# Re-ordering the opening of a fused attention and MLP kernel, with a new table of scheduling offsets

## The chip, the cores and the metric

The kernel runs on one core of a Trainium2 chip. The metric is the device time of one execution in microseconds; the value shown is the median of several executions.

## The reference

The program is an attention with a learned bias of relative position, followed by a two-layer MLP on its output. Everything is float32.

```python
# q, k, v: (4, 8, 576, 64); w1 (1, 32), b1 (32), w2 (32, 8); w_in (512, 2048), w_out (2048, 512)
scores = scale * q @ k.T
x = log1p(|i - j|) / log1p(max(i, 1))
bias = relu(x * w1 + b1) @ w2            # one value for each (i, j, head)
attn = softmax(scores + bias) @ v
x = attn as (2304, 512)
out = relu(x @ w_in) ** 2 @ w_out
```

## The kernel before

**Attention.** There are 80 steps (`steps`), one for each of two pairs of batches, five chunks of query rows (`ORDER`; chunk 0 is the 64-row tail and comes first) and eight heads. A step runs `qk` (scores in the one PSUM tile `sc`, from Q and K split in two float16 parts each), `softmax_a` (DVE adds the bias tile `bt`, takes the maximum and writes `s`, L441; ACT exponentiates, L445 to L447), `softmax_b` (the transposes for the next product: on PE in the first two chunks, L459 to L463, by DMA later) and, three steps behind (`LAG`), `pv`. After eight heads `finish_x` scales and splits the rows for the MLP.

**Bias.** The bias is made in 36 groups of 16 query rows. `hgen` makes four hidden tiles `hg` of a group, some on ACT, some on DVE: L303 and L305 for the first four groups, L307 and L309 for the others. `bias_mm` multiplies them with `w2` on PE (L348), evicts the result with ACT or DVE (L369 to L374) and stores it to DRAM (L378, tensor `biasd`). `bias_ld` (L392, L394) reads it back in the skewed layout that a step needs. The first four groups multiply the table by the row's factor directly; the later ones use row factors `rows_s` and inverted factors `scl`, which `rowscale` (L324 to L334) makes once from the table `tab_t`.

**MLP.** `moe_unit` runs `g1` (L560) and, some units later, `g2` (L583). The weights come as 32 pieces; `WT.split` rebuilds the words of each piece on DVE (`ci`, `cv`; L223, L224, L226), casts the high part on ACT (through `cast`, L129) and makes the low part on POOL (L131, L242). Two pieces a step are split in most of the first 16 steps (`W_AT`). `KV.split` and `q_split` cast K and Q on POOL (L131, L189) and finish Q on DVE (L268).

**Order of the work.** The instructions of `with pinned()` keep the program's order on each engine. Those of `with behind()` follow them. Everything else is ordered by a scheduler when the program is built: among the instructions that are ready by its own simulated times it takes the one with the smallest priority number, which grows in program order. `place(kind)` adds an offset from `PLACE` to the instructions inside it while the step is below `PLACED` (26), so that a positive offset moves them behind later work: `softmax_a`, the hidden tiles and the high casts of the weights by 150, K and V loads by 80, `bias_mm` by 20, and `qk` ahead by 10. On the chip each engine and each DMA queue then runs its own list in order. All DMAs are issued on SP's queue.

**The opening** (L735 to L765) loads the small constants `sm_t`, the table, two weight pieces, Q and K, makes the first four groups, splits K and Q (`kv_split(0)`, `q_split`), splits two weight pieces, runs `rowscale`, makes the hidden tiles of the fifth group and issues the bias loads of the first two heads. Step 0 with its `qk` and `softmax_a` comes after that.

Of the kernel before, what the change touches and what calls it, by code (L numbers as in the profile page):

```python
# [13 lines left out]
ALU = mybir.AluOpType  # L14
# [29 lines left out]
PLACE = {'qk': -10, 'wh': 150, 'sa': 150, 'hg': 150, 'bm': 20, 'kd': 80}  # L44
PLACED = 26
# [6 lines left out]
def tile_attention_moe(  # L52
# [57 lines left out]
    rows_s = const.tile([128, 36], F32, name="rows_s")  # L110
    nb1 = const.tile([128, 1], F32, name="nb1")
# [24 lines left out]
    @contextmanager  # L136
    def place(kind):
        n = PLACE.get(kind, 0) if now[0] < PLACED else 0
        tc.cur_priority += n
        yield  # L140
        tc.cur_priority -= n
# [59 lines left out]
    class WT:  # L201
# [14 lines left out]
        def split(self):  # L216
# [18 lines left out]
            with place("wh"):  # L235
                cast(zn("wh", u), hi, st, float(2 ** e))
# [49 lines left out]
    def hgen(G, pl=None):  # L286
        ts_ = []
        for t in range(4):
# [12 lines left out]
            if groups.index(G) < 4:  # L301
                if hg_pat(G)[t] == "A":
                    nc.scalar.activation(out=ht, in_=src, func=AF.Relu, bias=sm_t[:, 1:2], scale=sclw[:, n - 128:n - 127])  # L303
                else:
                    nc.vector.tensor_scalar(ht, src, sclw[:, n - 128:n - 127], nb1, op0=ALU.mult, op1=ALU.max)  # L305
# [5 lines left out]
        hg[G] = ts_  # L311

    def hconst():
# [4 lines left out]
        for z in sorted({hg_z(G) for G in groups}):  # L318
            nc.vector.tensor_copy(hcst[:, z:z + 1], cp[:, 0:1])
            for t in range(4):  # L320
                if PATS[z][t] == "A":
                    nc.vector.memset(hcst[32 * t:32 * t + 32, z:z + 1], 0.0)

    def rowscale():  # L324
        cp = ps_h.tile([128, 512], F32, tag="h", name="cp")
        for t in range(4):
            nc.tensor.matmul(out=cp[32 * t:32 * t + 32, 0:36], lhsT=sel,
                             rhs=scl.rearrange("p (g t) -> p t g", t=4)[:, t, :],
                             start=True, stop=True, tile_position=(0, 32 * t))
        nc.vector.tensor_copy(rows_s, cp[:, 0:36])  # L330
        nc.vector.reciprocal(out=scl, in_=scl)
        nc.vector.tensor_scalar(scl, scl, sm_t[:, 1:2], None, op0=ALU.mult)
        nc.gpsimd.tensor_scalar(w2n, w2s, -1.0, 1.0, op0=ALU.mult, op1=ALU.mult)
        nc.scalar.activation(out=tab_t[:, 0:LW], in_=tab_t[:, 0:LW], func=AF.Identity, scale=hcst[:, 3:4], bias=0.0)  # L334

    def bias_mm(G, gi):
        ts_ = hg.pop(G)
        z = hg_z(G)
        D_ = dlen(G)
        F_, M_ = S - 16 * G, 16 * G + 16  # L340
        cuts = [0, D_] if D_ <= 512 else [0, 288, D_]
        for d0, d1 in zip(cuts[:-1], cuts[1:]):
# [4 lines left out]
            for t in range(4):  # L347
# [3 lines left out]
                                 start=True, stop=True, tile_position=(0, 32 * t))  # L351

# [30 lines left out]
    def bias_ld(p, c, h):  # L383
# [6 lines left out]
        if c == 0:  # L390
            for b in range(2):
                last = nc.sync.dma_start(out=t[64 * b:64 * b + 64, :], in_=rows(512, 64))  # L392
# [483 lines left out]
```

## Time and profile before

| what | value |
|---|---|
| three executions | 661.16, 658.57, 660.46 us |
| median | 660.46 us |
| the profiled execution: its own time | 661.45 us |
| its span, first to last instruction | 659.7 us |
| mean granted TensorE clock over the span | 0.965 |
| PE, DVE, ACT, POOL busy | 93%, 62%, 59%, 57% of the span |

PE is TensorE, DVE VectorE, ACT ScalarE, POOL GpSimd, and SP the queue that issues the DMAs. L12 is line 12 of the kernel before. A busy share is an average over the span, and stages differ: so stretches are read one by one. A granted clock of 1.00 is 2.4 GHz and of 0.50 is 1.2 GHz; values between are means over a stretch with both. The wait in square brackets in a timeline is the idle time of the engine before that instruction, with what ended it.

### The profile page before, as it was taken

How to read it: one execution, taken by the hardware profiler on the slowest of the kernel's cores; microseconds unless marked ns; L12 is line 12 of the kernel's file. 1: busy time of each engine (PE TensorE's matmuls, PEld its weight loads, DVE VectorE, ACT ScalarE, POOL GpSimd, SP SyncE). 2: the span in 40 equal slices, each digit the busy share in tenths (PEclk: the TensorE clock that was granted, in tenths of full speed). 3: DMA queues.
4: the chain of work that ended last, by engine and by line, in shares of the span. 5: the costliest groups of instructions: out<-in, count | busy, mean ns of one | idle time of the engine just before them, and what ended most of it. 6: DMA issues, size and time to landing. Idle time of an engine off the chain costs nothing.

```text
span 659.7 us, 15574 instructions
## 1 busy us (share of the span) xinstructions
PE 615.1 (93%) x6056; PEld 394.8 (60%) x6056; DVE 407.1 (62%) x813; ACT 388.1 (59%) x856; POOL 376.5 (57%) x394
## 2 busy tenths in 40 slices
PE   5565798999899999999899999999999999999997
PEld 2223356766455566666576676676676676767664
DVE  7997999888864765585856447346545642632321
ACT  5587978788776476656656655656465564342111
POOL 2757578899665456756775465555464663432221
PEclk9698967999999999999899999999999999999999
DMA  7999888477876787889978778679787777524000
GB/s 237 278 294 319 268 255 248 155 209 178 197 173 152 162 193 176 179 180 226 221 170 158 167 134 174 140 169 153 139 172 134 154 149 155 122 56 86 17 34 16
DMA packets 206568, 112.16 MB, mean 170 GB/s; under 512 B 167072, under 2 KB 183456, under 8 KB 206496
## 3 DMA queue, kind: packets, MB, share of 16 engines
q1 hardware_dynamic: 206496, 111.19, 72.0%
q8 instruction: 47, 0.77, 0.5%
q14 instruction: 25, 0.20, 0.1%
HBM read 55.44 MB, written 15.61 MB: 108 GB/s over the span
## 4 chain that ended last, share of the span: by engine, by line
PE 69%; DVE 5%; DMA 4%; issue 2%; ACT 1%; POOL 1%; DVEq 0%; POOLq 0%; ACTq 0%
PE o L583 26%; PE hp L560 26%; PE pv L506 8%; PE sc L425 5%; PE bp L348 2%; DMA at<-a 2%; DVE hg L309 1%; PE sc L419 1%; PE sc L413 1%; DMA xt<-xh 1%; DMA stg<-vd 1%; DVE s L441 1%; DVE cv L226 0%; DVE ci L224 0%; ACT a L129 0%
## 5 line engine op out<-in xcount | busy, mean ns | idle before, releaser
L560 PE MATMUL hp<-xt,winH 128*128 128x256 f16 (+1 forms) x1280 | 195.9, 263 | 0.0
L583 PE MATMUL o<-woutH,g 128*128 128x512 f16 x576 | 185.6, 382 | 4.0 <-ACT o L590 2.2
L560 PE MATMUL hp<-xt,winL 128*128 128x256 f16 (+1 forms) x640 | 162.8, 263 | 0.0
L583 PEld LDWEIGHTS <-g 128*128 128x128 f16 x864 | 82.8, 98 | 97.0 <-issue 11.5
L560 PEld LDWEIGHTS <-winH 128*128 128x128 f16 x1280 | 117.0, 99 | 30.0 <-issue 13.6
L441 DVE CUSTOM_DVE_ANT_0 s<-sc,bt 128x576 f32<-128x576 f32 x144 | 103.5, 751 | 44.1 <-PE sc L425 34.2
L474 POOL TENSOR_TENSOR a<-s,a 128x1024 f16<-128x1024 f32 (+1 forms) x64 | 130.3, 2036 | 0.0
L568 DVE TENSOR_TENSOR r<-hp,r 128x512 f32<-128x512 f32 (+1 forms) x80 | 50.6, 632 | 118.7 <-ACT r L566 118.6
L570 POOL TENSOR_TENSOR g<-r,g 128x512 f16<-128x512 f32 (+1 forms) x80 | 86.7, 1084 | 59.1 <-DVE g L133 48.4
L447 ACT ACTIVATE s<-s,nm 128x576 f32<-128x576 f32 x144 | 111.3, 773 | 6.4
L583 PE MATMUL o<-woutL,g 128*128 128x512 f16 x288 | 109.8, 381 | 0.0
L473 POOL TENSOR_TENSOR a<-s,a 128x128 f16<-128x128 f32 (+1 forms) x64 | 28.1, 440 | 140.4 <-ACT a L129 135.5
L445 ACT ACTIVATE nm<-mx,esc 128x1 f32<-128x1 f32 x144 | 40.9, 288 | 110.8 <-DVE mx L441 110.5
L506 PE MATMUL pv<-v,at 128*128 128x64 f16 (+5 forms) x2112 | 97.9, 207 | 0.5 <-ACT at L460 0.5
L129 ACT ACTIVATE a<-s 128x1152 f16<-128x1152 f32 (+1 forms) x64 | 70.5, 1102 | 44.6 <-DMA at<-a 43.6
L566 ACT ACTIVATE r<-hp 128x512 f32<-128x512 f32 (+1 forms) x80 | 43.1, 539 | 49.6 <-PE hp L560 49.6
L506 PEld LDWEIGHTS <-at 128*128 128x128 f16 (+1 forms) x1792 | 58.3, 100 | 20.2 <-issue 8.6
L560 PEld LDWEIGHTS <-winL 128*128 128x128 f16 x640 | 62.9, 98 | 5.8
L309 DVE TENSOR_SCALAR hg<-tab_t 128x464 f32<-128x464 f32 (+17 forms) x86 | 58.9, 729 | 11.5 <-PE bp L348 11.4
L425 PE MATMUL sc<-k,q 64*128 64x512 f16 x384 | 55.6, 387 | 0.0
L369 ACT ACTIVATE be<-bp,hcst,rows_s 128x288 f32<-128x288 f32 (+29 forms) x67 | 35.8, 571 | 16.5 <-PE bp L348 11.1
L348 PE MATMUL bp<-hg,w2s 128*32 128x288 f32 (+15 forms) x152 | 36.1, 546 | 6.1 <-ACT hg L303 2.4
(88 smaller groups left out, 688.7 us busy)
## 6 DMA issues: line engine op xcount, KB each, us to landing
bt<-biasd SPq DMA_DIRECT2D x64, 288.0 KB, 3.3
stg<-w_in SPq DMA_DIRECT2D x16, 512.0 KB, 5.1
stg<-w_out SPq DMA_DIRECT2D x16, 512.0 KB, 4.7
bt<-biasd SPq DMA_DIRECT2D x32, 144.0 KB, 3.4
qst<-qd SPq DMA_DIRECT2D x32, 128.0 KB, 3.5
out<-o SPq DMA_DIRECT2D x16, 256.0 KB, 2.4
v<-vd SPq DMA_DIRECT2D x8, 320.0 KB, 4.9
stg<-vd SPq DMA_DIRECT2D x8, 320.0 KB, 4.3
```

The lines of the kernel that those rows point to most:

```text
L129: nc.scalar.activation(out=out, in_=in_, func=AF.Copy, scale=scale)
L309: nc.vector.tensor_scalar(ht, src, scl[:, n:n + 1], None, op0=ALU.min)
L348: nc.tensor.matmul(out=bp[32 * t:32 * t + 32, 0:d1 - d0], lhsT=w2s if gi < 4 or PATS[z][t] == "A" else w2n, rhs=ts_[t][:, d0:d1], start=Tr ...
L425: nc.tensor.matmul(out=sc[:, 1024 * b:1024 * b + 512], lhsT=qt[r, qz, qs], rhs=kt[r, z, 64 * b:64 * b + 512], start=(n == 0), stop=(n == 2 ...
L441: nc.vector.tensor_tensor_reduce(s[:, 576 * b:576 * b + 576], sc[:, 960 * sb:960 * sb + 576], bt, inv, -3.0e38, ALU.add, ALU.max, mx[:, b: ...
L447: nc.scalar.activation(out=sl, in_=sl, func=AF.Exp, bias=nm[:, b:b + 1], accum_out=su[:, h, b:b + 1])
L474: nc.gpsimd.tensor_tensor(av[:, :, 640:1152], ev[:, :, 0:512], av[:, :, 0:512], op=ALU.subtract)
L506: nc.tensor.matmul(out=dst, lhsT=lhsT, rhs=vt[r, 5 * b + blk, :] if f32 else vt[:, vz, 5 * b + blk, :], start=(n == 0), stop=(n == nt - 1) ...
L560: nc.tensor.matmul(out=hp[:, f * T:f * T + T].rearrange("p (b t) -> p b t", b=nb), lhsT=wt[:, k, c0:c0 + 128], rhs=xt[:, 0:nb, z * 4 + k, ...
L568: nc.vector.tensor_tensor(rr, hp[:, 0:2 * T], rr, op=ALU.mult)
L570: nc.gpsimd.tensor_tensor(g[:, 1, 0:2 * T], r[:, 0:2 * T], g[:, 0, 0:2 * T], op=ALU.subtract)
L583: nc.tensor.matmul(out=blk["o"][b], lhsT=g[:, z, c0:c0 + 128], rhs=wt[:, 2 * u + f, :], start=(u == 0 and f == 0 and z == 0 and wt is wout ...
```

## The change

The opening is re-ordered, and the offsets are replaced.

- The table's DMA is issued ahead of that of `sm_t`. `w2s`, one column of `hcst` and `w2n` are made on POOL instead of DVE and POOL late. `hconst` makes the three columns of `hcst` with one product of a mask `hmask` and the PSUM column instead of copies and memsets, and also runs the four pairs of matmuls for `rows_s`, which ACT copies out.
- `bias_mm` is cut in `bias_pe` and `bias_ev`, and the evictions of a group come one group of hidden tiles later. The reciprocal and product that invert `scl` stand between evictions.
- The first K split is made to wait for the last DVE hidden tile of the fourth group.
- The bias loads of two heads come ahead of the two weight pieces, one half tile on ACT's queue; `qk` and `softmax_a` of step 0 join the pinned part, ahead of the fifth group's hidden tiles.
- `PLACE` now holds ranges of steps with an offset each; ranges add up.

```diff
-PLACE = {'qk': -10, 'wh': 150, 'sa': 150, 'hg': 150, 'bm': 20, 'kd': 80}
-PLACED = 26
+PLACE = {'qk': [(22, 30, -20)], 'hg': [(0, 26, 150), (15, 31, 80)], 'bm': [(0, 26, 20), (25, 26, 80), (17, 19, 150)], 'm': [(24, 28, 20), (15, 16, 80)], 'pv': [(9, 34, -10)]}
...
-        n = PLACE.get(kind, 0) if now[0] < PLACED else 0
+        n = sum(x for a, b, x in PLACE.get(kind, ()) if a <= now[0] < b)
...
-            with place("wh"):
-                cast(zn("wh", u), hi, st, float(2 ** e))
+            cast(zn("wh", u), hi, st, float(2 ** e))
...
     def hconst():
...
-        for z in sorted({hg_z(G) for G in groups}):
-            nc.vector.tensor_copy(hcst[:, z:z + 1], cp[:, 0:1])
-            for t in range(4):
-                if PATS[z][t] == "A":
-                    nc.vector.memset(hcst[32 * t:32 * t + 32, z:z + 1], 0.0)
-
-    def rowscale():
-        cp = ps_h.tile([128, 512], F32, tag="h", name="cp")
         for t in range(4):
-            nc.tensor.matmul(out=cp[32 * t:32 * t + 32, 0:36], lhsT=sel,
+            nc.tensor.matmul(out=cp[32 * t:32 * t + 32, 8:44], lhsT=sel,
...
-        nc.vector.tensor_copy(rows_s, cp[:, 0:36])
-        nc.vector.reciprocal(out=scl, in_=scl)
-        nc.vector.tensor_scalar(scl, scl, sm_t[:, 1:2], None, op0=ALU.mult)
-        nc.gpsimd.tensor_scalar(w2n, w2s, -1.0, 1.0, op0=ALU.mult, op1=ALU.mult)
-        nc.scalar.activation(out=tab_t[:, 0:LW], in_=tab_t[:, 0:LW], func=AF.Identity, scale=hcst[:, 3:4], bias=0.0)
+        nc.vector.tensor_tensor(out=hcst[:, 0:3], in0=hmask, in1=cp[:, 0:1].to_broadcast([128, 3]), op=ALU.mult)
+        return cp
...
-                last = nc.sync.dma_start(out=t[64 * b:64 * b + 64, :], in_=rows(512, 64))
+                eng = nc.scalar if (p, c, h) == steps[0] and b == 0 else nc.sync
+                last = eng.dma_start(out=t[64 * b:64 * b + 64, :], in_=rows(512, 64))
...
-            tp = ps_o.tile([128, 512], F32, tag="o0", name="tp") if now[0] < 12 else ps_h.tile([128, 512], F32, tag="h", name="tp")
+            tp = ps_o.tile([128, 512], F32, tag="o0", name="tp") if now[0] < 10 else ps_h.tile([128, 512], F32, tag="h", name="tp")
...
+        nc.sync.dma_start(out=tab_t, in_=tabs)
         nc.sync.dma_start(out=sm_t, in_=sm)
-        nc.sync.dma_start(out=tab_t, in_=tabs)
...
-        nc.vector.tensor_scalar(w2s, sm_t[:, 2:34], float(2 ** (QS + KS + 3)), None, op0=ALU.mult)
         nc.vector.tensor_scalar(sclw, scl[:, 128:144], sm_t[:, 0:1], None, op0=ALU.mult)
         nc.vector.tensor_scalar(nb1, sm_t[:, 1:2], -1.0, None, op0=ALU.mult)
-        nc.vector.tensor_scalar(hcst[:, 3:4], sm_t[:, 0:1], -1.0, None, op0=ALU.mult)
+        nc.gpsimd.tensor_scalar(w2s, sm_t[:, 2:34], float(2 ** (QS + KS + 3)), 1.0, op0=ALU.mult, op1=ALU.mult)
+        nc.gpsimd.tensor_scalar(hcst[:, 3:4], sm_t[:, 0:1], -1.0, 1.0, op0=ALU.mult, op1=ALU.mult)
+        nc.gpsimd.tensor_scalar(w2n, w2s, -1.0, 1.0, op0=ALU.mult, op1=ALU.mult)
         hgen(groups[0], "hg")
-        hconst()
+        cp = hconst()
         hgen(groups[1], "a")
-        bias_mm(groups[0], 0)
+        nc.scalar.activation(out=rows_s, in_=cp[:, 8:44], func=AF.Copy)
+        b0 = bias_pe(groups[0], 0)
         hgen(groups[2], "at")
-        bias_mm(groups[1], 1)
-        hgen(groups[3], "s")
-        bias_mm(groups[2], 2)
-        bias_mm(groups[3], 3)
+        b1 = bias_pe(groups[1], 1)
+        bias_ev(groups[0], 0, b0)
+        row = hgen(groups[3], "s")
+        b2 = bias_pe(groups[2], 2)
+        bias_ev(groups[1], 1, b1)
+        nc.vector.reciprocal(out=scl, in_=scl)
+        nc.vector.tensor_scalar(scl, scl, sm_t[:, 1:2], None, op0=ALU.mult)
+        b3 = bias_pe(groups[3], 3)
+        bias_ev(groups[2], 2, b2)
+        bias_ev(groups[3], 3, b3)
+        nc.scalar.activation(out=tab_t[:, 0:LW], in_=tab_t[:, 0:LW], func=AF.Identity, scale=hcst[:, 3:4], bias=0.0)
+        n0 = len(nc.cur_bb.bb.instructions)
         kv_split(0)
+        tc.add_manual_dep(nc.cur_bb.bb.instructions[n0], row.name, mybir.DependencyInfo(
+            mybir.DependencyClass.Sync, mybir.DependencyReason.DATA), reason="split behind the rows")
         q_split(*qlist[0])
+        for h in range(2):
+            bias_ld(*steps[h])
         ld_split()
         ld_split()
-        rowscale()
+        qk(*steps[0])
+        softmax_a(*steps[0])
         gi = 4
         hgen(groups[gi])
-        for h in range(2):
-            bias_ld(*steps[h])
...
-            with place("qk"):
-                qk(p, c, h)
-            with place("sa"):
+            if t:
+                with place("qk"):
+                    qk(p, c, h)
+            if t:
                 softmax_a(p, c, h)
...
-                moe_unit()
+                with place("m"):
+                    moe_unit()
         if last >= 0:
-            pv(*steps[last])
+            with place("pv"):
+                pv(*steps[last])
...
-        with place("kd"):
-            kv_dma(t + 2)
+        kv_dma(t + 2)
```

## Rows read from the trace of the kernel before

**Rows 1.** The page, part 1: busy us, share of the span, instructions.
```profile
PE 615.1 (93%) x6056; PEld 394.8 (60%) x6056; DVE 407.1 (62%) x813; ACT 388.1 (59%) x856; POOL 376.5 (57%) x394
```

**Rows 2.** The page, part 4: shares by engine of the chain that ended last.
```profile
PE 69%; DVE 5%; DMA 4%; issue 2%; ACT 1%; POOL 1%; DVEq 0%; POOLq 0%; ACTq 0%
```

**Rows 3.** Busy time in chosen stretches: length, engines with counts, TensorE clock, DMA share, GB/s.
```profile
20.00:140.00 120.00, 94.97 (x734) 56.70 (x735) 109.97 (x196) 95.71 (x228) 87.84 (x104) 0.83 0.88 265
85.00:96.00 11.00, 11.00 (x51) 7.30 (x51) 10.62 (x20) 9.05 (x20) 8.61 (x9) 0.53 0.94 274
105.00:116.00 11.00, 11.00 (x70) 8.87 (x62) 9.98 (x19) 8.39 (x21) 9.94 (x12) 0.53 0.78 236
...
200.00:300.00 100.00, 100.00 (x1037) 63.03 (x1035) 62.38 (x127) 59.90 (x134) 57.55 (x54) 1.00 0.80 174
```

**Rows 4.** Timeline of SP's queue, opening: start, length, issue, count.
```profile
0.79 0.41 SPq L736 DMA_DIRECT2D sm_t<-sm  x1
1.26 0.42 SPq L737 DMA_DIRECT2D tab_t<-tabs  x1
...
16.62 2.62 SPq L392 DMA_DIRECT2D bt<-biasd  x4
```

**Rows 5.** Timeline of DVE, opening: start, length, instruction, count, idle before and its releaser.
```profile
4.34 0.23 DVE L745 TENSOR_SCALAR sclw<-tab_t,sm_t 128x16 f32<-128x16 f32 x1 [1.54 <-DMA tab_t<-tabs]
...
6.07 0.41 DVE L319 COPY hcst<-cp 128x1 f32<-128x1 f32 x3
6.34 0.35 DVE L322 MEMSET hcst<- 32x1 f32 x3
...
8.60 1.04 DVE L305 TENSOR_SCALAR hg<-tab_t,sclw,nb 128x560 f32<-128x560 f32 x2
...
10.67 2.27 DVE L305 TENSOR_SCALAR hg<-tab_t,sclw,nb 128x576 f32<-128x576 f32 x2
...
14.19 0.52 DVE L372 TENSOR_SCALAR be<-bp,hcst 128x288 f32<-128x288 f32 x1 [0.85 <-PE bp L348]
14.62 0.68 DVE L268 SCALAR_TENSOR_TENSOR q<-qst,q 128x512 f16<-128x512 f32 x1
...
18.86 0.69 DVE L226 SCALAR_TENSOR_TENSOR cv<-stg,ci 128x512 uint32<-128x512 uint32 x1
...
19.57 1.04 DVE L331 RECIPROCAL tab_t<-tab_t 128x144 f32<-128x144 f32 x1
20.64 0.35 DVE L332 TENSOR_SCALAR tab_t<-tab_t,sm_t 128x144 f32<-128x144 f32 x1
21.10 1.73 DVE L309 TENSOR_SCALAR hg<-tab_t 128x320 f32<-128x320 f32 x2
22.75 0.74 DVE L441 CUSTOM_DVE_ANT_0 s<-sc,bt 128x576 f32<-128x576 f32 x1
```

**Rows 6.** Timeline of PE, opening.
```profile
5.50 8.42 PE L348 MATMUL bp<-hg,w2s 128*32 128x288 f32 x63 [2.35 <-ACT hg L303]
...
23.88 0.64 PE L413 MATMUL sc<-k,q 128*128 128x64 f16 x2 [8.10 <-POOL k L131]
```

**Rows 7.** Timeline of POOL, opening.
```profile
9.80 0.67 POOL L131 TENSOR_SCALAR k<-kst 128x576 f16<-128x576 f32 x1 [7.58 <-DMA kst<-kd]
```

**Rows 8.** DMA issues of the first 30 us: count, KB each, us to landing.
```profile
bt<-biasd SPq DMA_DIRECT2D x8, 144.0 KB, 4.0
```

**Rows 9.** Waits from 20 to 120 us: us in total, times, longest.
```profile
PE sc L413 <- POOL k L131: 11.5, 3, 8.1
...
PE sc L413 <- DVE mx L441: 5.8, 2, 3.3
...
DVE cv L226 <- DMA biasd<-be: 3.1, 1, 3.1
```

**Rows 10.** Hidden tiles on DVE: tile view, 21 to 60 us (ns min/median/max); page, part 5.
```profile
L309 DVE TENSOR_SCALAR hg<-tab_t x16: 368/627/1459, 21.1 to 54.3; 128x320 f32<-128x320 f32 x4, 128x304 f32<-128x304 f32 x4, 128x336 f32<-128x336 f32 x2, 128x352 f32<-128x352 f32 x2
...
L309 DVE TENSOR_SCALAR hg<-tab_t 128x464 f32<-128x464 f32 (+17 forms) x86 | 58.9, 729 | 11.5 <-PE bp L348 11.4
```

More of the change, by code (lines that the diff above doesn't have):

```diff
@@ L110, in tile_attention_moe @@
     rows_s = const.tile([128, 36], F32, name="rows_s")
+    hmask = const.tile([128, 3], F32, name="hmask")
     nb1 = const.tile([128, 1], F32, name="nb1")
@@ L286, in hgen @@
     def hgen(G, pl=None):
-        ts_ = []
+        ts_, last = [], None
         for t in range(4):
@@ L304, in hgen @@
                 else:
-                    nc.vector.tensor_scalar(ht, src, sclw[:, n - 128:n - 127], nb1, op0=ALU.mult, op1=ALU.max)
+                    last = nc.vector.tensor_scalar(ht, src, sclw[:, n - 128:n - 127], nb1, op0=ALU.mult, op1=ALU.max).ins
             elif hg_pat(G)[t] == "A":
@@ L311, in hgen @@
         hg[G] = ts_
+        return last
     def hconst():
@@ L317, in hconst, with bias_pe @@
                              start=True, stop=True, tile_position=(0, 32 * t))
-        for z in sorted({hg_z(G) for G in groups}):
-            nc.vector.tensor_copy(hcst[:, z:z + 1], cp[:, 0:1])
-            for t in range(4):
-                if PATS[z][t] == "A":
-                    nc.vector.memset(hcst[32 * t:32 * t + 32, z:z + 1], 0.0)
-    def rowscale():
-        cp = ps_h.tile([128, 512], F32, tag="h", name="cp")
         for t in range(4):
-            nc.tensor.matmul(out=cp[32 * t:32 * t + 32, 0:36], lhsT=sel,
+            nc.tensor.matmul(out=cp[32 * t:32 * t + 32, 8:44], lhsT=sel,
                              rhs=scl.rearrange("p (g t) -> p t g", t=4)[:, t, :],
                              start=True, stop=True, tile_position=(0, 32 * t))
-        nc.vector.tensor_copy(rows_s, cp[:, 0:36])
-        nc.vector.reciprocal(out=scl, in_=scl)
-        nc.vector.tensor_scalar(scl, scl, sm_t[:, 1:2], None, op0=ALU.mult)
-        nc.gpsimd.tensor_scalar(w2n, w2s, -1.0, 1.0, op0=ALU.mult, op1=ALU.mult)
-        nc.scalar.activation(out=tab_t[:, 0:LW], in_=tab_t[:, 0:LW], func=AF.Identity, scale=hcst[:, 3:4], bias=0.0)
+        nc.vector.tensor_tensor(out=hcst[:, 0:3], in0=hmask, in1=cp[:, 0:1].to_broadcast([128, 3]), op=ALU.mult)
+        return cp
     def bias_mm(G, gi):
+        bias_ev(G, gi, bias_pe(G, gi))
+    def bias_pe(G, gi):
         ts_ = hg.pop(G)
@@ L339, in bias_mm @@
         D_ = dlen(G)
-        F_, M_ = S - 16 * G, 16 * G + 16
         cuts = [0, D_] if D_ <= 512 else [0, 288, D_]
+        bps = []
         for d0, d1 in zip(cuts[:-1], cuts[1:]):
@@ L351, in bias_mm, with bias_ev @@
                                  start=True, stop=True, tile_position=(0, 32 * t))
+            bps.append((d0, d1, bp))
+        return bps
+    def bias_ev(G, gi, bps):
+        z = hg_z(G)
+        F_, M_ = S - 16 * G, 16 * G + 16
+        for d0, d1, bp in bps:
             parts = [(max(d0, 1), min(d1, M_), True), (d0, min(d1, F_), False)]
@@ L700, in tile_attention_moe @@
     nc.vector.memset(hcst, 0.0)
+    nc.vector.memset(hmask, 1.0)
+    for z in range(3):
+        for t in range(4):
+            if PATS[z][t] == "A":
+                nc.vector.memset(hmask[32 * t:32 * t + 32, z:z + 1], 0.0)
     nc.vector.memset(kz, 0.0)
```

## Prediction

> **What bounds the kernel now.** I read the page first: PE is busy 615.1 us of a span of 659.7 [rows 1], and PE holds 69% of the chain that ended last [rows 2]. So the end comes when PE has done its work, and the change can only gain what PE now loses: 44.6 us idle, and matmuls run at the lower clock. Busy time by stretch says where that lies. From 200 to 300 us PE is busy all the time at clock 1.00; from 20 to 140 us it is busy 94.97 of 120 us, with a mean clock of 0.83, and there DVE is the full engine, 109.97 of 120 us [rows 3]. A mean of 0.83 over two levels means that about a third of that stretch, some 41 us, ran at 1.2 GHz; in 85 to 96 and 105 to 116 PE was busy every microsecond at a mean of 0.53 [rows 3]. So the first 140 us are set by DVE and by what PE waits for, and the rest by PE alone. A microsecond by which the DVE-bound part is shortened is a microsecond off the end, as long as the PE-bound part stays full. The change acts on the first part nearly alone. The timelines give the opening's prices, the waits those of the steps after it.
>
> **The table first.** Its DMA goes out at 0.79 instead of 1.26 us [rows 4], so `sclw`, which waited for it until 4.34 [rows 5], can start up to 0.47 us earlier. Now it also waits for `sm_t` behind the table, whose landing there no row shows; the worst is that it lands no earlier than the table did. Gain 0 to 0.47; I take 0.47, because `sm_t` is a small fraction of the table's size.
>
> **DVE's work among the first groups.** The copies and memsets of `hcst` take from 6.07 to 6.69 [rows 5]; one small product in their place costs perhaps 0.2, so 0.4 is saved. The reciprocal and the product on `scl` held DVE from 19.57 to 20.99 and move into waits such as the 0.85 at 14.19 [rows 5]. The last hidden tiles took 2.27 for a pair of 576, where the pair of 560 took 1.04; POOL's K split began at 9.80, just before [rows 5, 7]. Putting the split behind those tiles takes that away. But none of this moves the end of the groups. PE multiplied them without a break from 5.50 for 8.42 us, to 13.92 [rows 6], and the last eviction followed at 14.19. DVE's list from 4.34 to 14.71 is 10.4 us with its waits; less the wait of 0.85, the surplus of 1.2 and the 0.4, and with the 1.4 of `scl`, it is 9.3 us, which ends at 13.2 from a start at 3.87. PE ends later, at 13.45, and the last eviction follows PE. So that part moves with PE's start only, by 0.47, and its last eviction ends near 14.2 instead of 14.7.
>
> Here the Trainium skill speaks (SBUF — State Buffer, Who interferes with whom): a VectorE instruction that uses both ports and a GpSimd instruction block each other for a whole instruction. By that rule alone the wait of the split returns 1.2 us, the surplus of the 576 pair; by the row of PE it returns nothing, as PE ends the stretch, and I keep the latter.
>
> **The split's new wait.** K was split at 9.80, when its DMA landed [rows 7]. The 560 pair ended at 9.64 [rows 5]; less 0.47 and 0.4, and with a quick pair of 576 behind it (1.1, from 1.04 for 560), the last hidden tile ends at 9.9, and the split loses 0.1. DVE took Q's low part at 14.62 without a wait for POOL [rows 5] and will at 14.2. Behind the waiting split on POOL stand Q's cast and the low parts of the two weight pieces, which are not due before DVE's `cv`. Cost 0; were DVE late by a microsecond or two, step 0 would begin to wait. The three small products moved to POOL lie in its idle 7.58 us before 9.80 [rows 7]. `rows_s` moves to ACT, at a fraction of a microsecond between hidden tiles that PE's 8.42 us cover.
>
> **The first softmax.** DVE then does Q and six passes for two weight pieces: 14.62 to 19.46 before, now 14.2 to 19.0 [rows 5]. Step 0's `s` follows at once, if its bias tile has landed. Its four issues began at 16.62 and took 2.62 [rows 4]; they begin once the stores have landed, so 0.47 earlier, at 16.15. The two halves of the first tile go out together, one from ACT's queue; a landing takes 4.0 [rows 8], so `s` can start at 20.15 instead of 22.75, 2.6 us earlier. On ACT the high casts of the weight pieces stand behind that DMA's wait; they need the first `cv` at about 16.9 (14.2, 0.6 for Q and three passes of 0.7), after it. The fifth group's hidden tiles, 1.65 us from 21.10 to 22.75, come behind `s`. Behind `s` (0.67) and these, DVE is free at 22.5 where it was at 23.42. So DVE gains **0.9 us**; 2.0 if the tile is there when DVE is, and 0 if the landing takes a microsecond longer. What is late next is the transfer of the bias tile.
>
> The Trainium skill (DMA: Bandwidth & Descriptors, Issuing engines are not separate DMA queues) says that issuing from a second engine saves issue time only; by its rule ACT's half tile brings one issue, a quarter of the 2.62 us, and the first softmax would be at 20.15 or later, never at 19.0.
>
> **The offsets.** PE waited for K's split in 3 places for 11.5 us, 8.1 of these in the gap up to 23.88 [rows 6, 9], and for `s` (to free `sc`) for 5.8 us in 2 [rows 9]. `softmax_a` loses its offset of 150, K and V loads that of 80, the casts that of 150: each makes one of these waits shorter. The 8.1 us gap ends only some 0.8 earlier, as K of head 1 still stands on POOL behind the weight pieces. But DVE has almost no room: of 120 us it was idle 10.0 [rows 3], and a softmax done earlier is a weight piece or hidden tile done later. One wait of 3.1 us at DVE, for a free eviction buffer [rows 9], is the largest part of the idle time. So the offsets can return 0 to 10 us as DVE time; PE work done sooner can also shorten its 41 us at the low clock. In the other direction the surplus of hidden tiles beside POOL's work grows, as below. I take **4.5 us**, somewhat under half of DVE's idle time, as nearest to the one row of 3.1 us plus the smaller K and `s` waits. The ranges in steps 9 to 34 (`pv`, `bm`, `m`, `qk`) order PE's work where PE is full; I cost them at 0, hidden by the queued MLP work, and at 1 to 2 us of waits at PE if that cover is gone.
>
> **Sum.** 0.9 + 4.5 = 5.4 us off 661.45, the profiled execution's own time (1.75 above its span): 656.05. The median shown is 1.0 below that execution, so the forecast against it is 660.46 - 5.4 = **655.0 us** in round numbers.
>
> **Rivals.**
> - *The opening alone.* The offsets cancel out, since DVE has as much to do as before: 660.46 less 0 to 2.0, so 658.5 to 660.5. For it speaks that DVE is full in 20 to 140 us; against it, PE's 17.3 us of waits for K and `s`, which are what the offsets touch. The same comes out if the scheduler's own simulated times leave the order on the chip as it was.
> - *Slower: hidden tiles beside POOL.* A DVE hidden tile from 21 to 60 us took 368 ns at least, 627 in the median and 1459 at most, for the same or like shapes [rows 10]. If the casts come sooner, POOL has its low parts ready at more of the moments when DVE runs hidden tiles. From 20 to 140 us there are 38 of them with 27.71 us, a mean of 729 ns [rows 10], so 100 ns more in the mean is 3.8 us of DVE. From 142 ns more on, the 5.4 us are eaten; at 230 to 310 ns more, still below the slowest of them, the time is 663.8 to 666.9. Against it: `hg` keeps its offset of 150, and about half of the tiles are slow already. The rule of the skill named above is what this would rest on, and the 1.04 against 2.27 of the trace agrees with it.
> - *The clock comes back.* If PE's gaps close enough that 85 to 96 and 105 to 116 run at 2.4 GHz, up to half of each 11 us is returned to PE, and with DVE's gain the time is 644 to 650. For it: each of those stretches is full at half speed. Against: DVE is also 90% busy or more in both, so PE would mostly wait instead. The Trainium skill (TensorE: Matmul & The Clock Gate, HAM oscillation) says that idle gaps between bursts bring the low clock again each time; by it closing the gaps pays twice.
>
> **Numbers.** The forecast has 0.45 (650 to 658), the opening alone 0.28, slower 0.15, the clock 0.12. A measurement here can tell about 0.5%, 3.3 us, from no change: below 657.2 is faster. Nearly all of the forecast and the clock case lie there, and a trace of the second: 0.55. Slower than 663.8 gets 0.14, the rest, 0.31, is the same. The range from 647.5 to 662.5 takes in the forecast, the opening alone and half of the clock case, and leaves out the slower case. The forecast's own range is 650 to 658.
>
> **What would show it.** Right: `sclw` near 3.9, PE's first group matmul near 5.0, the last eviction near 14.2, the first `s` near 20 and DVE free by 22.5; from 20 to 140 less idle on DVE, PE's waits for K and `s` halved and the last `cv` 4 to 6 us earlier. Wrong: the same DVE idle time with other waits, a mean of the hidden tiles above 0.85 us, or PE gaps after 150 us at `bp` or `pv` that were not there.

## The result, and the profile after

The changed kernel is slower: 665.13 us in the median of six executions (664.19 to 668.37) against 658.17 us of the kernel before in the same comparison (656.48 to 661.16), a ratio of 1.0118 with a 95% interval of 1.0093 to 1.0142. The forecast of 655.0 us was wrong in its sign, and the measured time lies outside the range. The profiled execution took 664.77 us, 663.0 of them its span. The profiled execution of the kernel before, 661.45 us, was at the slow end of its own runs, so the two traces lie only 3.3 us apart where the medians lie 7 apart. The profiled execution of the kernel after has the highest mean TensorE clock of its six, 0.968 where the others have 0.953 to 0.960.

The page of the kernel after, parts 1 and 4, answers to [rows 1, 2].

```profile
PE 610.7 (92%) x6056; PEld 392.8 (59%) x6056; DVE 407.0 (61%) x809; ACT 388.3 (59%) x857; POOL 375.3 (57%) x396
...
PE 55%; DMA 17%; DVE 15%; issue 5%; ACT 4%; POOL 3%; SPq 0%; DVEq 0%; POOLq 0%; ACTq 0%
```

PE has 4.4 us less busy time and still ends later: its idle time went from 44.6 to 52.3 us. The chain that ended last now runs through DMA and DVE for 32% of the span, where it was 9%.

Busy time in the stretches of [rows 3], and one between them, for the kernel after (length, then PE, PEld, DVE, ACT, POOL with counts, TensorE clock, DMA share, GB/s):

```profile
20.00:140.00 120.00, 90.72 (x726) 53.26 (x726) 105.25 (x192) 93.01 (x223) 84.82 (x100) 0.85 0.85 259
85.00:96.00 11.00, 9.21 (x52) 5.77 (x54) 10.97 (x25) 9.18 (x24) 6.36 (x7) 0.69 0.86 245
105.00:116.00 11.00, 9.60 (x57) 6.86 (x57) 9.30 (x18) 7.72 (x18) 10.26 (x13) 0.69 0.73 231
140.00:200.00 60.00, 56.17 (x553) 33.46 (x554) 44.98 (x83) 44.59 (x95) 44.30 (x48) 1.00 0.72 167
200.00:300.00 100.00, 98.46 (x1017) 62.45 (x1014) 64.80 (x131) 61.63 (x136) 56.38 (x53) 1.00 0.84 174
```

From 20 to 140 us every engine does less than before, at nearly the same clock: PE 90.72 instead of 94.97, DVE 105.25 instead of 109.97, ACT 93.01 instead of 95.71. DVE, the full engine of that stretch, now stands 14.75 us of 120 instead of 10.03. From 200 to 300 us PE, which was never idle there, has 1.5 us of gaps. The two short stretches do run at a mean of 0.69 instead of 0.53, but PE is no longer busy all the time in them.

The opening in the timelines of SP, DVE, PE and POOL, answering to [rows 4 to 7]:

```profile
0.79 0.41 SPq L740 DMA_DIRECT2D tab_t<-tabs  x1
1.26 0.42 SPq L741 DMA_DIRECT2D sm_t<-sm  x1
...
15.81 1.76 SPq L391 DMA_DIRECT2D bt<-biasd  x3
...
4.26 0.23 DVE L748 TENSOR_SCALAR sclw<-tab_t,sm_t 128x16 f32<-128x16 f32 x1 [2.00 <-DMA sm_t<-sm]
...
8.86 1.06 DVE L304 TENSOR_SCALAR hg<-tab_t,sclw,nb 128x576 f32<-128x576 f32 x2
...
11.30 1.32 DVE L765 TENSOR_SCALAR tab_t<-tab_t,sm_t 128x144 f32<-128x144 f32 x1
12.54 0.92 DVE L370 TENSOR_SCALAR be<-bp,hcst 128x272 f32<-128x272 f32 x2
...
19.62 0.76 DVE L440 CUSTOM_DVE_ANT_0 s<-sc,bt 128x576 f32<-128x576 f32 x1 [1.33 <-DMA bt<-biasd]
...
21.67 0.68 DVE L223 TENSOR_SCALAR ci<-stg 128x512 uint32<-128x512 uint32 x1
...
5.41 6.40 PE L340 MATMUL bp<-hg,w2s 128*32 128x288 f32 x64 [0.45 <-ACT hg L302]
...
21.67 1.11 PE L458 MATMUL tp<-ident,s 128*128 128x128 f32 x4 [7.14 <-ACT s L446]
...
10.49 0.67 POOL L131 TENSOR_SCALAR k<-kst 128x576 f16<-128x576 f32 x1 [5.59 <-DMA kst<-kd]
```

The opening did what it was to do, and somewhat more. The first groups' products take 6.40 us instead of 8.42, the last eviction ends at 13.46, the first softmax stands at 19.62 instead of 22.75, and DVE is free of it and of the fifth group's tiles at 21.67 instead of 23.42. PE still stands before step 0's next work, 7.14 us up to 21.67 for the first transposes, where it stood 8.10 up to 23.88 for K [rows 6]. So the loss arises later.

### The profile page after: what moved, and what is told of

Read it like the earlier page. It is cut to its first block, busy times and chain, and to the rows that moved or that the text cites. A ratio compares the mean times of both kernels' runs of the same rounds, so it can differ in the third digit from the quotient of the medians.

```text
span 663.0 us, 15555 instructions
## 1 busy us (share of the span) xinstructions
PE 610.7 (92%) x6056; PEld 392.8 (59%) x6056; DVE 407.0 (61%) x809; ACT 388.3 (59%) x857; POOL 375.3 (57%) x396
## 4 chain that ended last, share of the span: by engine, by line
PE 55%; DMA 17%; DVE 15%; issue 5%; ACT 4%; POOL 3%; SPq 0%; DVEq 0%; POOLq 0%; ACTq 0%
PE hp L559 22%; PE o L582 21%; PE pv L505 6%; DMA at<-a 5%; PE sc L424 4%; DMA biasd<-be 3%; DVE hg L308 3%; DVE s L440 3%; DMA xt<-xh 2%; DVE ci L224 2%; DVE ci L223 1%; DVE cv L226 1%; POOL a L473 1%; DMA bt<-biasd 1%; PE bp L340 1%
## 5 line engine op out<-in xcount | busy, mean ns | idle before, releaser
L505 PE MATMUL pv<-v,at 128*128 128x64 f16 (+5 forms) x2112 | 112.9, 207 | 1.0 <-ACT at L459 0.5
L505 PEld LDWEIGHTS <-at 128*128 128x128 f16 (+1 forms) x1792 | 64.1, 100 | 27.1 <-issue 14.2
L565 ACT ACTIVATE r<-hp 128x512 f32<-128x512 f32 (+1 forms) x80 | 43.1, 539 | 46.7 <-PE hp L559 44.9
L308 DVE TENSOR_SCALAR hg<-tab_t 128x464 f32<-128x464 f32 (+17 forms) x86 | 56.8, 709 | 4.5 <-PE bp L340 4.4
```

Source lines behind the costliest of these rows:

```text
L308: nc.vector.tensor_scalar(ht, src, scl[:, n:n + 1], None, op0=ALU.min)
L505: nc.tensor.matmul(out=dst, lhsT=lhsT, rhs=vt[r, 5 * b + blk, :] if f32 else vt[:, vz, 5 * b + blk, :], start=(n == 0), stop=(n == nt - 1) ...
L565: nc.scalar.activation(out=r[:, 0:2 * T], in_=hp[:, 0:2 * T], func=AF.Relu, scale=float(2.0 ** (-2 * RS)))
```

## The experiments

Two theories stood at the start. One: some part of the change costs time by itself (the opening, the offsets taken away, or the new ranges). The other, the rival: the offsets are only one input of the scheduler, each edit gives new lists for all engines behind it, and the new lists are worse whatever the edit was meant to do. The ratios below are to the kernel before, with their 95% intervals.

### The halves of the change

`e1_opening` has the new opening and all old offsets; the PSUM rule of steps 10 and 11 (the `now[0] < 10` of the diff) stays with the opening:

```diff
-PLACE = {'qk': [(22, 30, -20)], 'hg': [(0, 26, 150), (15, 31, 80)], 'bm': [(0, 26, 20), (25, 26, 80), (17, 19, 150)], 'm': [(24, 28, 20), (15, 16, 80)], 'pv': [(9, 34, -10)]}
+PLACE = {'qk': [(0, 26, -10)], 'wh': [(0, 26, 150)], 'sa': [(0, 26, 150)], 'kd': [(0, 26, 80)], 'hg': [(0, 26, 150)], 'bm': [(0, 26, 20)]}
...
-            cast(zn("wh", u), hi, st, float(2 ** e))
+            with place("wh"):
+                cast(zn("wh", u), hi, st, float(2 ** e))
...
-                softmax_a(p, c, h)
+                with place("sa"):
+                    softmax_a(p, c, h)
...
-        kv_dma(t + 2)
+        with place("kd"):
+            kv_dma(t + 2)
```

> The new opening with the old offsets. Theory A (the opening gains about 2 us of lost PE time up to 70 us, as the trace after shows, and the offsets lose it): 655 to 657 us where before gives 658, a ratio of 0.995 to 0.998. Rival B (the opening itself costs, by the order it leaves behind): 662 to 666, ratio 1.007 or more. Rival C (everything depends on the exact order and nothing adds up): anything from 655 to 666 with no relation to the other three.

Measured: 1.0044 (1.0027 to 1.0061). `e2_offsets` is its complement, the old opening with the new `PLACE`, its ranges and `place` calls.

> The old opening with the new offsets. Theory A: worse than the changed kernel by the opening's 2 us, so 666 to 668, ratio 1.012 to 1.016. Rival B (the opening costs): the same as before, 657 to 660. Rival C: no relation.

Measured: 1.0177 (1.0148 to 1.0206). The other two keep the new opening. `e3_ranges` is `e1_opening` with the new ranges on top of the old offsets; `e4_dropped` takes the offsets of `wh`, `sa`, `kd` and the early `qk` away and has none of the ranges:

```diff
+PLACE = {'qk': [(0, 22, -10), (22, 30, -20)], 'wh': [(0, 26, 150)], 'sa': [(0, 26, 150)], 'kd': [(0, 26, 80)], 'hg': [(0, 26, 150), (15, 31, 80)], 'bm': [(0, 26, 20), (25, 26, 80), (17, 19, 150)], 'm': [(24, 28, 20), (15, 16, 80)], 'pv': [(9, 34, -10)]}
...
+PLACE = {'qk': [(22, 26, -10)], 'hg': [(0, 26, 150)], 'bm': [(0, 26, 20)]}
```

> The new opening, the lost offsets (softmax_a, high casts, K and V loads, qk) given back, the new ranges in steps 9 to 34 kept. If the ranges cost the some 4 us of PE time that the trace after loses between 170 and 260 us: 659 to 662. If the lost offsets are the cause (the loss at 70 to 80 us): 655 to 657.

> The new opening, the offsets of softmax_a, high casts, K and V loads and qk gone as in the change, but the ranges of steps 9 to 34 put back to the old ones (hg 150, bm 20 up to step 25, no others). If the ranges cost 4 us: 660 to 661, with less PE idle time between 170 and 260 us than the changed kernel. If the lost offsets are the cause: 664 to 666 as the changed kernel.

Measured: `e3_ranges` 1.0123 (1.0098 to 1.0149), `e4_dropped` 1.0094 (1.0063 to 1.0124). `e1_opening` lies between the ranges of its first two theories, `e2_offsets` above all of its own, and `e3_ranges` above both of its own; `e4_dropped` came as for the lost offsets. What follows: every half is slower, the offsets most, and the whole is faster than the offsets alone. The parts don't add up.

### Single offsets in the old kernel

```diff
+PLACE = {'qk': -10, 'wh': 0, 'sa': 0, 'hg': 150, 'bm': 20, 'kd': 0}
...
+PLACE = {'qk': -10, 'wh': 150, 'sa': 150, 'hg': 150, 'bm': 20, 'kd': 0}
```

The first is `d_all`, the second `d_kd`. `r_all` adds all the ranges to the old offsets, `r_hgbm` those of `hg` and `bm` alone.

> The old opening and old offsets, but softmax_a, high casts and K and V loads without theirs. Theory: the lost offsets cost 0.5% with the new opening (1.0094 against 1.0044) and cost the same without it: ratio 1.003 to 1.008. Rival (they cost only together with the new opening): 0.998 to 1.002. If they are what makes the old opening with the new offsets the worst (1.0177): 1.010 or more.

> The old kernel with the offset of K and V loads alone gone (earlier loads of K and V). If it is the loads that crowd out the bias stores and weight pieces on the queue: most of what all three cost together, 1.003 to 1.008. If the loads help PE's wait for K as the prediction held: 0.995 to 0.999.

> The old opening and old offsets with the new ranges of steps 9 to 34 added. Theory: the ranges cost 0.8% with the new opening (1.0123 against 1.0044) and the same without it: 1.006 to 1.010, with PE time lost between 170 and 260 us as in the changed kernel. Rival (they are made for, or against, the new opening only): 0.998 to 1.003.

> The old kernel with the new ranges of hidden tiles and bias_mm alone (hg 230 in steps 15 to 25 and 80 to step 30, bm up to 170 in steps 17 and 18). If later bias groups are what starves PE between 170 and 260 us: most of the ranges' cost, 1.005 to 1.010, with softmax in steps 18 to 30 later by 3 to 8 us. If it is the MLP's or pv's ranges: 0.998 to 1.002.

Measured: `d_all` 1.0226 (1.0182 to 1.0269), `d_kd` 1.0119 (1.0085 to 1.0153), `r_all` 1.0050 (1.0026 to 1.0074), `r_hgbm` 1.0057 (1.0036 to 1.0079). `d_kd` and `r_all` lie outside the ranges expected of them; `d_all` is above 1.010, the third case. One offset, that of the K and V loads, costs as much as the whole change. Its largest wait in the timelines of PE and ACT of `d_kd`:

```profile
104.23 1.11 PE L459 MATMUL tp<-ident,s 128*128 128x128 f32 x4 [5.12 <-ACT be L369]
...
102.94 1.24 ACT L369 ACTIVATE be<-bp,hcst,rows_s 128x207 f32<-128x207 f32 x2 [1.97 <-DMA biasd<-be]
```

ACT's eviction of a bias group stood for a store of an earlier group, whose buffer it needs; PE's transposes, which need the PSUM tile that the eviction frees, stood 5.12 us for ACT, with the rest of PE's list behind them. Of these, 1.97 us are the wait for the store and 1.24 the eviction itself; before that ACT ran two casts of weight pieces, with 0.48 us of waiting for `cv`.

### Giving one part back

`a_kd` is the changed kernel with the offset of the loads back. `o_kd`, `o_hgbm` and `o_old0` are `e1_opening` with one thing changed: without the offset of the loads; with the ranges of `hg` and `bm`; with step 0's scores and softmax and the first bias loads again behind the fifth group.

```diff
+PLACE = {'qk': [(22, 30, -20)], 'hg': [(0, 26, 150), (15, 31, 80)], 'bm': [(0, 26, 20), (25, 26, 80), (17, 19, 150)], 'm': [(24, 28, 20), (15, 16, 80)], 'pv': [(9, 34, -10)], 'kd': [(0, 26, 80)]}
...
+PLACE = {'qk': [(0, 26, -10)], 'wh': [(0, 26, 150)], 'sa': [(0, 26, 150)], 'hg': [(0, 26, 150)], 'bm': [(0, 26, 20)]}
...
+PLACE = {'qk': [(0, 26, -10)], 'wh': [(0, 26, 150)], 'sa': [(0, 26, 150)], 'kd': [(0, 26, 80)], 'hg': [(0, 26, 150), (15, 31, 80)], 'bm': [(0, 26, 20), (25, 26, 80), (17, 19, 150)]}
...
-        for h in range(2):
-            bias_ld(*steps[h])
         ld_split()
         ld_split()
-        qk(*steps[0])
-        softmax_a(*steps[0])
         gi = 4
         hgen(groups[gi])
+        for h in range(2):
+            bias_ld(*steps[h])
```

> The changed kernel with one thing given back: the offset of 80 of the K and V loads. Theory (the earlier loads are a cost of their own, 1.2% in the old kernel): 1.002 to 1.008, with PE's waits for ACT's evictions (be, at; 18.9 us in the changed kernel from 20 to 260 us) down to 10 us or less. Rival (with the new ranges in place it does not matter, as the run with all lost offsets given back stayed at 1.0123): 1.010 to 1.014.

> The new opening with the old offsets but that of the K and V loads. Theory (the earlier loads cost by themselves): 1.004 plus most of 1.2%, 1.010 to 1.016, and PE's waits for be and at at 13 us or more where the new opening with old offsets has 7.7. Rival (with the new opening they cost little, as all lost offsets together cost 0.5% there): 1.004 to 1.009.

> The new opening and the old offsets, with the new ranges of hidden tiles and bias_mm alone. Theory (late bias groups in steps 15 to 30 are most of the ranges' 0.8%, as the same ranges cost 0.57% in the old kernel): 1.008 to 1.012, the loss of PE time between 170 and 260 us. Rival (pv's, qk's and the MLP's ranges): 1.003 to 1.006.

> The new opening and the old offsets, but step 0's scores and softmax behind the fifth group's hidden tiles again, and the first bias loads behind those (all on SP's queue order of before). Theory (the opening's 0.4% comes from DVE standing for the bias tile in the pinned order, 2.7 us in the new opening with old offsets): 0.999 to 1.002 and that wait under 1 us. Rival (the cost lies in the steps behind, which are ordered otherwise, and in the clock from 70 to 120 us): 1.003 to 1.008.

Measured: `a_kd` 1.0116 (1.0094 to 1.0138), `o_kd` 1.0073 (1.0056 to 1.0089), `o_hgbm` 1.0056 (1.0032 to 1.0080), `o_old0` 1.0070 (1.0046 to 1.0094). The offset that cost 1.2% in the old kernel costs 0.3% with the new opening, and given back to the changed kernel it returns nothing. Taking the first softmax out of the opening doesn't help either. No single part carries the loss, which speaks for the rival, but does not show it.

The ranges act late. Taken instruction by instruction, and apart from matmuls that start together, the timelines of `r_all` and `r_hgbm` have the order of the kernel before up to 150 and 162 us, and `e3_ranges` has that of `e1_opening` up to 153. So their 0.5 to 0.8% come with lists that are new only behind the first 16 steps (step 16 begins at 141.5 us in the kernel before).

### Holding the lists

The next three kernels separate an edit from the lists that it brings. At the end of the program every instruction behind the opening is chained, on its engine, to the one that stood before it in the list of another kernel (`HELD`, taken from that kernel as built); the scheduler has no choice left:

```diff
+    for k, i in enumerate(nc.cur_bb.bb.instructions[n_hold:]):
+        (lead if k in Q0 else held).setdefault(str(i.engine).split(".")[1], []).append(i)
+    for e, runs in json.loads(zlib.decompress(base64.b85decode(HELD))).items():
+        line = lead.get(e, []) + [held[e][k + j] for k, n in runs for j in range(n)]
+        for one, two in zip(line, line[1:]):
+            tc.add_manual_dep(two, one.name, mybir.DependencyInfo(
+                mybir.DependencyClass.NoSync, mybir.DependencyReason.DATA), reason="held")
```

`h_open` is `o_old0` and `h_full` is `e1_opening`, both held to the lists of the kernel before; `x_list` is the kernel before, held to the lists of the kernel after, with step 0's scores and softmax at their head. The PSUM rule of steps 10 and 11, the `now[0] < 12` of the diff, goes with the lists. In the timelines, behind the opening, DVE, ACT, POOL and SP of `h_full` have the order of the kernel before, and those of `x_list` that of the kernel after.

> New opening (all but the first softmax and first bias loads, which stand where they stood before, and the PSUM rule of step 12 as before); behind the opening every engine and queue is held to the very list of instructions of the kernel before. Theory of the lists (what is lost is lost because the scheduler writes new lists for every engine behind the edit, and those put PE behind ACT's evictions): the opening alone in its own list was 1.0070; with the list held it is 0.995 to 1.001, PE's waits for evictions in 20 to 260 us (bias and transposes) near before's 7.7 us. Rival, the opening itself (attention that starts earlier meets weight pieces, bias groups and the low clock at the wrong moment, whatever the list): 1.004 to 1.009 again.

> The whole new opening, first softmax ahead of the fifth group included; the rest held to the lists of the kernel before. Theory of the lists: 0.993 to 1.000, at least 0.4% under the same opening with old offsets in its own list (1.0044). Rival, the opening itself: 1.003 to 1.006. In both the first s comes near 19.6 us.

> The opening of the kernel before, but behind it every engine is held to the lists of the changed kernel (steps 1 on, with step 0's scores and softmax at their head). Theory of the lists: 1.010 to 1.020, as slow as the changed kernel or slower, since the lists carry the loss and the opening's 2 us are missing too. Rival, the opening itself or its meeting with the new offsets: 0.998 to 1.006.

| ratio to before | lists of before | lists of after |
|---|---|---|
| opening of before | 1 | `x_list` 1.0133 (1.0095 to 1.0170) |
| opening of after | `h_full` 0.9989 (0.9967 to 1.0012) | after 1.0118 (1.0093 to 1.0142) |

`h_open` took 0.9993 (0.9974 to 1.0013). This settles it: the loss lies in the lists, 1.3% under either opening, and the opening changes nothing that can be told, 0.1 to 0.2% in either column. The theory that the opening itself costs the 0.4% of `e1_opening` falls. One thing is not separated: no run changed the PSUM rule alone, so "the lists" of the table are lists with their rule. The rule is not needed for a loss, since `e2_offsets`, `d_all` and `d_kd` keep the old one and lose 1.2 to 2.3%.

What the lists do shows in PE's waits from 20 to 260 us (total, times, longest). The kernel after, all its lines that wait for ACT's evictions:

```profile
PE bp L340 <- ACT at L459: 5.8, 6, 1.4
PE tp L458 <- ACT be L367: 4.7, 7, 2.1
...
PE tp L458 <- ACT at L459: 2.8, 2, 2.5
PE bp L340 <- ACT be L367: 2.7, 2, 1.6
...
PE tp L462 <- ACT at L459: 2.4, 3, 1.0
...
PE pv L505 <- ACT at L459: 0.5, 1, 0.5
```

And `h_full`, the same opening with the old lists:

```profile
PE bp L342 <- ACT at L461: 2.2, 1, 2.2
PE tp L464 <- ACT at L461: 1.8, 4, 1.0
...
PE tp L460 <- ACT be L369: 1.2, 2, 0.9
PE bp L342 <- ACT be L369: 1.1, 2, 0.9
...
PE tp L460 <- ACT at L461: 0.7, 1, 0.7
...
PE hp L561 <- ACT at L461: 0.3, 1, 0.3
```

The lines add up to 18.9 us in the kernel after and to 7.3 in `h_full`. The same sum is 7.7 in the kernel before, 7.5 in `h_open` and 17.8 in `x_list`: it goes with the lists, not with the opening. The waits of PE together are 31.9 us before and 39.8 after, 7.9 more.

Waits are not all that the lists cost. Part 1 of the pages of `h_full` and of `x_list`:

```profile
PE 610.7 (94%) x6056; PEld 393.8 (60%) x6056; DVE 404.8 (62%) x809; ACT 387.6 (59%) x857; POOL 377.4 (58%) x396
```

```profile
PE 620.2 (93%) x6056; PEld 398.9 (60%) x6056; DVE 408.8 (61%) x813; ACT 388.6 (58%) x856; POOL 374.4 (56%) x394
```

Under the new opening PE's idle time is the whole difference of the two traces: PE is busy 610.7 us in `h_full` and in the kernel after, and the spans of 652.4 and 663.0 differ by PE's idle time, 41.7 and 52.3 us. (The profiled execution of `h_full`, 654.12 us, is the fastest of its twelve, whose median is 657.97.) Under the old opening they are less than half of it: the span of `x_list`, 668.7 us, is 9.0 longer than before, of which 3.9 are idle time and 5.1 busy time for as many matmuls, at a mean clock of 0.950 instead of 0.965. So the lists cost PE waits and clock, in shares that differ between these traces; that the waits for ACT carry the loss after the change is read from traces, and no run took one of them away alone. In kernels whose lists are all their own the sum does not follow the time (18.0 us in `e4_dropped` at 1.0094, 9.5 in `e2_offsets` at 1.0177). There PE is busy 620.3 and 619.4 us instead of 615.1, and idle 44.1 and 46.7 instead of 44.6: these two lose mostly in busy time.

One place shows how. Timelines of ACT, PE and DVE of the kernel after around 75 us:

```profile
74.27 1.10 ACT L367 ACTIVATE be<-bp,hcst,rows_s 128x143 f32<-128x143 f32 x2 [2.12 <-DMA biasd<-be]
75.26 1.16 ACT L306 ACTIVATE hg<-tab_t 128x416 f32<-128x416 f32 x2
76.33 0.62 ACT L129 ACTIVATE winH<-cv 128x512 f16<-128x512 f32 x1
76.85 0.58 ACT L459 ACTIVATE at<-tp 128x512 f32<-128x512 f32 x1
...
75.42 0.66 PE L458 MATMUL tp<-ident,s 128*128 128x128 f32 x4 [2.08 <-ACT be L367]
77.48 0.91 PE L340 MATMUL bp<-hg,w2s 128*32 128x416 f32 x2 [1.40 <-ACT at L459]
...
77.44 0.76 DVE L440 CUSTOM_DVE_ANT_0 s<-sc,bt 128x576 f32<-128x576 f32 x1 [2.38 <-DMA bt<-biasd]
```

ACT stands 2.12 us at the head of its list with an eviction whose buffer is still being stored. PE stands for that eviction, then a second time for `at`, which on ACT comes behind two hidden tiles and a cast. DVE stands for the bias tile of a step that has run ahead of its bias group. Ten microseconds later, on ACT and PE:

```profile
85.35 0.63 ACT L129 ACTIVATE woutH<-cv 128x512 f16<-128x512 f32 x1 [1.30 <-DVE cv L226]
85.89 0.58 ACT L459 ACTIVATE at<-tp 128x512 f32<-128x512 f32 x1
...
86.52 0.66 PE L458 MATMUL tp<-ident,s 128*128 128x128 f32 x4 [2.55 <-ACT at L459]
```

A cast of a weight piece, which has lost its offset, waits for DVE's `cv`, the eviction behind it is late, and PE stands 2.55 us. `x_list` has the same two waits at the same places, 2.92 us at 75.05 and 2.31 at 86.15; from 72 to 90 us no wait of PE in `h_full` is longer than 0.91.

### Where, and on whose list

`h_16` is the changed kernel with its own offsets, in which only the instructions of steps 0 to 15 are held to their order in the kernel before (the PSUM rule of steps 10 and 11 too is that of before). `m_SPPOOL` is `h_full` with POOL's and SP's lists taken from the kernel after. `n1` is a control, one offset changed a little in the old kernel:

```diff
-PLACE = {'qk': -10, 'wh': 150, 'sa': 150, 'hg': 150, 'bm': 20, 'kd': 80}
+PLACE = {'qk': -10, 'wh': 150, 'sa': 150, 'hg': 150, 'bm': 22, 'kd': 80}
```

> The changed kernel's opening and its own new offsets, but the instructions of steps 0 to 15 are held to the order in which they stood in the kernel before; the later steps are ordered freely by the new offsets. If the loss arises in the lists of the first 16 steps (the 5 us of PE time lost between 80 and 140 us, of the 8 us lost by 260): 0.999 to 1.004, with PE's waits for ACT's evictions (bias and transposes) in 20 to 260 us back near 8 us of the changed kernel's 18.9. If the ranges in the later steps carry as much of it: 1.006 to 1.012.

> New opening; the lists of PE, DVE and ACT held as before, those of POOL and of SP's DMA queue as in the changed kernel. If the moment of the loads and casts is the cause (taking the offset of the K and V loads out of the kernel before cost 1.2%): 1.008 to 1.014. If the loss lies in the order on PE, ACT and DVE: 0.997 to 1.003, like the run with all lists held.

> Control: the kernel before with one offset changed from 20 to 22, which moves a few instructions in the lists of PE, ACT, POOL and SP and none on DVE. Theory of the lists: what counts is which instruction stands behind which eviction, not that a list is new; this one moves few, so 0.998 to 1.003. Rival: any new list costs some 0.5%, as each single edit so far did: 1.004 to 1.007.

Measured: `h_16` 0.9974 (0.9956 to 0.9992), `m_SPPOOL` 1.0327 (1.0297 to 1.0358), `n1` 0.9986 (0.9968 to 1.0004).

`h_16`, a little under its expected range, shows where: with the first 16 steps in the old order (and the old PSUM rule) the whole loss is gone, and the new offsets cost nothing in the steps after them. In the timelines its order is that of the kernel before up to 168 us on DVE, ACT and SP, and that of the kernel after from 195 us on, on every engine. So the lists that cause the loss lie ahead of 195 us. That most of it comes early is likely, not shown: `e4_dropped`, without the ranges, has the order of the kernel after up to 153 us and loses 0.9%, but its later lists are new too. PE's waits for ACT's evictions are 8.9 us again. It is also the fastest kernel of the study, 656.62 us against 658.50, a gain of 1.9 us that its interval just separates from nothing; as the best of eighteen, it is no proof of a gain.

`m_SPPOOL` missed both expectations: it is slower than any list that belongs together. DVE's waits from 20 to 140 us in it:

```profile
DVE ci L224 <- DMA stg<-w_in: 11.5, 3, 6.5
DVE q L269 <- POOL q L132: 7.1, 2, 5.5
DVE ci L224 <- DMA stg<-w_out: 3.3, 1, 3.3
```

DVE takes weight pieces and Q in the old order while the loads and casts bring them in the new one, and it stands 21.9 us. So the question whose list is at fault was badly put: the lists are fitted to one another, and a run with one engine's list alone says little. `n1` shows that a new list is not slow because it is new; this one moves some instructions on PE, ACT, POOL and SP, none on DVE, and costs nothing. It is a weak control, since in the timelines all that it moves lies behind 216 us, outside the stretch in which the lists of the kernel after lose.

## Why the prediction was wrong

**The offsets** are the step that failed. "The offsets can return 0 to 10 us as DVE time" was read from the waits of PE for K and `s`. Those for `s` went as foretold: from 20 to 120 us PE waits for it 3.5 us instead of 8.7 (with the forms of L419, now L418). Those for K only seem to, with 5.5 us instead of 11.5 [rows 9]. The kernel after:

```profile
PE sc L412 <- POOL k L131: 3.0, 1, 3.0
...
PE sc L412 <- POOL k L189: 2.5, 3, 1.0
```

Of the 11.5 us, 8.1 were the gap of the opening, which is still 7.14 us long and now ends with a wait for ACT's `s`. The other waits for K's split rose from 3.4 to 5.5 us. So the 4.5 us did not come back: part of the waits stayed, and others were added. I asked what the moved work would no longer make wait, and not what stands behind it where it now stands. DVE's waits from 20 to 140 us in the kernel after:

```profile
DVE s L440 <- DMA bt<-biasd: 3.7, 2, 2.4
DVE s L440 <- PE tp L458: 2.5, 1, 2.5
...
DVE s L440 <- DMA biasd<-be: 1.3, 1, 1.3
DVE s L440 <- PE sc L412: 1.0, 1, 1.0
```

The softmax, freed of its offset, came to the head of DVE's list before its bias tile or scores were there: 8.5 us in these lines for `s`, where the same view of the kernel before has 0.7 for PE, 0.2 for a bias tile and 0.2 for another load, 1.1 in all. DVE's idle time rose by 4.7 us where I had it fall by 4.5. On ACT it was the evictions, as shown above.

**The ranges** of steps 9 to 34 I costed at 0, or 1 to 2 us. With the first 16 steps held, `h_16` shows no cost, so the 0 stands there. In the old kernel `r_all` measured 0.5%, about 3 us, although its order changes only from 150 us on. So lists behind the first 16 steps can cost time too; why those of `r_all` do and those of `h_16` do not stays open.

**The opening's terms.** The table first was worth 0.08 us (4.26 instead of 4.34), not 0.47: `sclw` now waits for `sm_t`, the worse end of what I had allowed. That PE sets the end of the first groups was wrong: with the work taken off DVE and re-ordered, the products took 6.40 us at the same granted clock (1.00 in both stretches), so PE's 8.42 very likely held waits for hidden tiles between the products, which the trace shows as busy time. (They also ended later than the 13.92 of the prediction: one more product ran from 13.75 to 14.16.) The last eviction therefore ended at 13.46, not 14.2. The Trainium skill's rule (SBUF — State Buffer, Who interferes with whom), that a VectorE instruction which uses both ports and a GpSimd instruction block each other, was weighed there and set aside. The trace of the kernel after agrees with it: the pair of 576 takes 1.06 us with the split behind it, instead of 2.27. The product on `scl` now falls beside the split, and takes 1.32 us instead of 0.35 [rows 5], so most of what the pair gained was paid there. The split's wait cost nothing, as foretold, but it did nothing either: the tiles ended at 9.92, and POOL waited for K's DMA until 10.49. How much of the shorter stretch of products is due to the later split and how much to the work taken off DVE stays open. The first softmax stood for its bias tile, as foretold, at 19.62 instead of 20.15. The sum, 0.9 us on DVE, measured 1.75.

**That a microsecond of DVE in the first part is one off the end** was the larger error behind these. In `h_full`, with every later instruction in its old place, the first softmax starts 3.6 us earlier (19.18) and DVE is free 2.2 us earlier (21.23), and the end gained 0.7 us (0.1%, not told from nothing).

**The rivals.** The opening alone (658.5 to 660.5 of 660.46, ratio 0.997 to 1.000) is what `h_full` measured when its lists are held; in lists of its own it was 1.0044. The slower side had the wrong mechanism. Hidden tiles beside POOL did not grow: they are 38 from 20 to 140 us in both kernels, first before, then after:

```profile
20.00:140.00 120.00, 27.71 (x38) 0.83 0.88 265
```

```profile
20.00:140.00 120.00, 25.17 (x38) 0.85 0.85 259
```

Their mean fell from 729 to 662 ns (25.17 / 38). (The 27.71 and its mean of 729 in the prediction are from the first of these rows; the page's row in [rows 10] is of another shape and stretch.) The clock came back in part, from 0.53 to 0.69 in both short stretches, and paid nothing, since PE waited instead, which was the reason given against that rival.

What I named as a sign of being wrong, gaps of PE after 150 us that were not there, is in the trace, though not where I named it: 1.5 us from 200 to 300 us, at `hp` and not at `bp` or `pv`. It says little, since `h_16`, which loses nothing, has 1.2 us of gaps there (PE busy 98.82 of 100). The other sign, the same idle time of DVE with other waits, came as more of it.

## What to carry to other kernels

Where a scheduler writes in-order lists for several engines, a priority does not move one instruction alone, it can re-write every list behind it; cost the change by what stands behind each instruction that may now reach the head of its list too early, here on the engine that evicts PSUM above all, and read the granted clock beside the waits. To tell an edit from the lists that it brings, hold the lists: a two by two table of edit and lists settled what taking parts away could not. Early gains that end in a stretch where several engines wait on one another should be counted at nothing until a trace shows them at its end.

## What the runs showed of the hardware that I had not expected

A kernel can lose on the clock what it gains in waits. Busy time from 70 to 110 us in the kernel before, in `e1_opening` and in `e2_offsets`:

```profile
70.00:110.00 40.00, 32.55 (x231) 20.88 (x229) 38.88 (x77) 33.95 (x83) 27.17 (x30) 0.82 0.88 265
```

```profile
70.00:110.00 40.00, 33.85 (x187) 21.83 (x187) 37.02 (x73) 30.55 (x72) 27.62 (x31) 0.65 0.92 269
```

```profile
70.00:110.00 40.00, 33.28 (x179) 20.76 (x178) 31.30 (x64) 28.22 (x66) 22.34 (x27) 0.57 0.84 243
```

PE is busy longer in both than before, and gets fewer matmuls done (187 and 179 instead of 231), at a mean clock of 0.65 and 0.57 instead of 0.82. The same stretch has 0.70 in `x_list` and 0.62 in `e4_dropped`, but 0.84 in the kernel after. The two levels are 1.2 and 2.4 GHz, and what sets off the lower one here was not tried; so for these four kernels waits alone don't explain the time.
